# Converting weight pairs in one piece ahead of the sums, in the first block of a two-layer MLP, and a border cast behind two copies

## The chip, the cores and the metric

The kernel runs on one core of a Trainium2 chip. The metric is the device time of one execution in microseconds. The engines are named by what they do: TensorE (PE in the rows; PEld are its weight loads), VectorE (DVE), ScalarE (ACT), GpSimd (POOL) and SyncE (SP), which here only issues DMAs.

## What is computed

The input is a sequence of 2 x 3008 tokens with 256 features. A spectral layer (a real Fourier transform along the sequence, a complex 256 x 256 product, a soft threshold, the inverse transform) is followed by two MLP layers, each with 2048 hidden features:

```python
def _moe_ref(x, w_in, w_out):
    h = x @ w_in
    g = h * (1.0 / (1.0 + np.exp(-1.702 * h)))
    return (g @ w_out).astype(np.float32)

x = attn_out.reshape(B * S, D)          # 6016 x 256
x = _moe_ref(x=x, **moe_kwargs)
return _moe2_ref(x=x, **moe2_kwargs)    # the same with h * sigmoid(h)
```

The MLP weights arrive as 64-bit floating point numbers, seen as int64. The chip's engines do not compute in that type, so the kernel converts them with shifts and masks.

## The kernel before, in words

**Stages.** The forward transform, the middle product and the inverse transform come first; then the MLP. The conversion of the weights is spread over all of them. The tokens are cut into blocks of 1024 (the last has 896), and a block into two halves h of 512. `group(l, i, p)` does layer l, block i and a pair p of chunks of 128 hidden features, p = 0 to 7. Every fp32 operand of a product is split into a high part (rounded) and a remainder, and each product is three matmuls of 512 columns: high x high, high x remainder, remainder x high.

**A group.** The first layer's product of a pair is done with seven products in place of eight, by the Strassen-Winograd scheme: sums of input pieces (`xprep` 0 to 6) times sums of weight pieces (slots 0 to 6 of `w_in`). In the text they go by their piece of the input: X0 and Y1, then Z3 and X4, then X5 and Z6, then X2; X, Z, Y are three PSUM banks, of four. ScalarE copies a bank to SBUF (L791, L801, L803), VectorE adds another bank to that (L793, L809, L812), and the four results (y1 to y4) go through a gate: the activation (L775), a cast to the high part (L777), and `rest`, the remainder (L782), on VectorE for one of the four and on GpSimd for three. The second layer's products (L744, `out_next`) take these with a lag of four, that is a group later. Seven first-layer products and eight second-layer ones, of three matmuls each, make 45 matmuls a group. X5 and Z6 write banks that L801 and L803 must have read.

**Converting a pair of weights.** `cv_load` starts the DMA of a raw pair (L144, L145 or L148); there is one raw buffer. `cv_bits` begins with ScalarE (L157) and puts five steps of VectorE on the list `fill`, L162 to L166; L164 and L166 read the raw buffer, L166 last. `pump(k)` issues k of the steps, all without a number. `settle` adds the two parts (L219, on GpSimd). A kept pair of `w_in` is then placed in the next group by `place_in`: four sums on VectorE (L194 to L197, into the one buffer `tmp`), then two `put`s, each a cast on ScalarE and a remainder on GpSimd (both at L98 and L99): the pair itself (`cv_a`, 384 columns) and the sums (`tmp`, 512). A pair of `w_out` has one cast and one remainder (`place_out`). Pairs that cannot be kept yet are written to DRAM (`spilled`) and fetched again later (`cv_ld`).

**Which groups convert.** `WEIGHTS` lists the pairs with the mark `kept`; ten are converted before the MLP. In the first block of layer 1 (l = 0, i = 0) the groups p = 1 to 6 convert one pair each, all six kept: three of `w_in` and three of `w_out`. In blocks 1 to 4 the groups p = 1, 3, 5 and 6 convert one each (`kr`), sixteen in all, none kept. In the first block's groups p = 0 to 4 a spilled pair of `w_out` is placed too.

**What sets the order.** `hook(h)`, h = 1 to 6, is called at fixed points of a group and inserts what belongs there: at 1 the conversion's start (L157), at 2 and 3 placings of fetched weights, at 3 (or 1) the placing of converted ones, at 4 the rest of `fill` and the next raw load, at 5 a fetch, at 6 `settle`. From the group (0, 0, 1) on the order of the program is the order on every engine; group (0, 0, 0) and what lies beside it are ordered by a scheduler. Each engine, and each DMA queue, works in order. In group p = 0 of every block `xprep` 4, 6 and 5 (a cast on ScalarE, L692, and a remainder on VectorE, L695) are done in the group itself, at hooks 1, 2 and 3; the first four were done in the group before.

The lines at which the steps of the conversion are split up:

```python
        rest(nc.gpsimd, *gate(0, 0, y1))
        hook(2)
        pump(3)
```

Of the kernel before, what the change touches and what calls it, by code (L numbers as in the profile page):

```python
# [56 lines left out]
def spectral_mlp_kernel(ctx, tc, xin, m0, mfwd, minv, wc, bias, w_in1, w_out1, w_in2, w_out2, outT):  # L57
    nc = tc.nc
# [6 lines left out]
    def E(site, i=0):  # L65
        s = CFG.get(site, DEF[site])
        return {"V": nc.vector, "P": nc.gpsimd}[s[i % len(s)]]
# [135 lines left out]
    wib_p = []  # L203
# [12 lines left out]
    def settle():  # L216
        pump()
        for u, (a, c) in bits:
            E('cva', u[2]).tensor_add(a, a, c)  # L219
            if not u[3]:  # L220
                spilled[u[:3]] = d = dram_p.tile([P, 2 * CU], F32, name=f"w_{u[0]}{u[1]}_{u[2]}")
                nc.sync.dma_start(out=d, in_=a)
        fresh = [(u, a) for u, (a, _) in bits if u[3]]
        done, added[:] = added[:], fresh
        bits[:] = []
        return done

    def window(k, done, now=False):
        for u, a in done:
            if u[0] == "in":  # L230
                for part in place_in(u[1], u[2], a, E('pil', u[2]), sums_tmp):
                    if now:
                        for f in part:
                            f()
                    else:
                        fill.extend(part)
            else:
                place_out(u[1], u[2], a, E('pol', u[2]))
        for _ in range(min(k, len(loaded))):
            u, raw = loaded.pop(0)  # L240
            bits.append((u, cv_bits(raw)))
# [518 lines left out]
    def group(l, i, p, hook):  # L760
        t0, n = blocks[i]
        func = AF.Silu if l else AF.Gelu_apprx_sigmoid
        w = w_in[l, p]

        y = [[yt[:, mm, t0 + h * n : t0 + (h + 1) * n] for h in range(2)] for mm in range(2)]

        def prod(ps, s, k, first=True):

            xh, xl = xb[l, i, k]
            a, z = w[:, 0, s], w[:, 1, s]  # L770
            for m, (st, mv) in enumerate(((a, xh), (a, xl), (z, xh))):
                nc.tensor.matmul(ps, st, mv, start=first and m == 0, stop=m == 2, skip_group_check=True)  # L772

        def gate(row, h, g, src=None):
            nc.scalar.activation(g, g if src is None else src, func)  # L775
            gh = slot(1, F32R, "g")[:, :n]
            nc.scalar.copy(gh, g)  # L777
            return row, h, g, gh

        def rest(eng, row, h, g, gh):  # L780
            gl = slot(1, F32R, "g")[:, :n]
            eng.tensor_sub(gl, g, r32(gh))  # L782
            pend.append((l, i, p, row, h, gh, gl))

        (y1, y3), (y2, y4) = y
        begun = (l, i, p) != (0, 0, 0)
        X, Z, Y = (bank(0, "x")[:, :n] for _ in range(3))
        prod(X, 0, 0)  # L790
        nc.scalar.copy(y1, X)  # L791
        prod(Y, 1, 1)
        nc.vector.tensor_add(y1, y1, Y)  # L793
        hook(1)
        if begun:
            out_next()
        rest(nc.gpsimd, *gate(0, 0, y1))
        hook(2)
        pump(3)
        prod(Z, 3, 2)  # L800
        nc.scalar.copy(y2, Z)  # L801
        prod(X, 4, 3, False)
        nc.scalar.copy(y3, X)  # L803
        hook(3)
        if begun:
            out_next()
            out_next()
        prod(X, 5, 4, False)
        nc.vector.tensor_add(y2, y2, X)  # L809
        g22 = gate(1, 1, y2)  # L810
        prod(Z, 6, 6, False)
        nc.vector.tensor_add(y3, y3, Z)  # L812
        rest(nc.vector, *g22)
        g12 = gate(0, 1, y3)
        rest(nc.gpsimd, *g12)
        hook(4)
        if begun:
            out_next()
        hook(5)
        prod(X, 2, 5, False)  # L820
        rest(nc.gpsimd, *gate(1, 0, y4, X))
        hook(6)
# [25 lines left out]
    puts = []  # L848
# [12 lines left out]
    for at, (l, i, p) in enumerate(seq):  # L861
# [10 lines left out]
        def hook(h):  # L872
            if more:
                if h in (1, 2):
                    for x in ((0,), (1, 2))[h - 1]:
                        xprep(*nxt, x)
                if h == 3:
                    xprep(*nxt, 3, 1)
                if h == 4:
                    xprep(*nxt, 3, 2)  # L880
            if p == 0 and h < 4:
                xprep(l, i, {1: 4, 2: 6, 3: 5}[h])
            if h == 1 and p == NPR - 2 and (l, i) != (1, last):
                xsums(*nxt)
            if h == (3 if len(done) < 2 else 1):
                window(0, done, True)
                done[:] = []
            if h == 1:
                window(k, ())
            if h in (2, 3):  # L890
                moved(h)
            if h == 5:
                fetched[:] = fetch_for(at + 1)
            if h == 4:
                pump()
                cv_load(1 - len(loaded))
            if h == 6:
                done.extend(settle())
                done.extend(added)
                added[:] = []  # L900
# [159 lines left out]
```

## Time and profile before

| what | value |
|---|---|
| runs | 1248.66, 1251.43, 1253.36 us; median 1251.43 |
| the profiled execution | 1253.26 us, its span 1251.5 us |
| TensorE busy | 1187.8 us (95% of the span) |
| ScalarE, VectorE, GpSimd busy | 775.6, 698.2, 587.8 us |
| mean granted TensorE clock | 0.985 of full speed |

The span is the time from the first to the last instruction; the profiled execution's time is 1.8 us longer. Busy shares are means over stages with different limits: the transforms take some 220 us, the rest is the MLP. A busy TensorE is not TensorE at its peak, since matmuls overlap and their ends are modelled.

### The profile page before, as it was taken

How to read it: one execution, taken by the hardware profiler on the slowest of the kernel's cores; microseconds unless marked ns; L12 is line 12 of the kernel's file. 1: busy time of each engine (PE TensorE's matmuls, PEld its weight loads, DVE VectorE, ACT ScalarE, POOL GpSimd, SP SyncE). 2: the span in 40 equal slices, each digit the busy share in tenths (PEclk: the TensorE clock that was granted, in tenths of full speed). 3: DMA queues.
4: the chain of work that ended last, by engine and by line, in shares of the span. 5: the costliest groups of instructions: out<-in, count | busy, mean ns of one | idle time of the engine just before them, and what ended most of it. 6: DMA issues, size and time to landing. Idle time of an engine off the chain costs nothing.

```text
span 1251.5 us, 14934 instructions
## 1 busy us (share of the span) xinstructions
PE 1187.8 (95%) x5220; PEld 969.8 (77%) x5220; DVE 698.2 (56%) x1034; ACT 775.6 (62%) x1481; POOL 587.8 (47%) x465
## 2 busy tenths in 40 slices
PE   7879888777999999999999999999999999999998
PEld 4868678556787887887878987878888888888897
DVE  7899999866735646447446463352352442623522
ACT  3555433656766766767667777666675665765764
POOL 4585553555544444445455774433333333333342
PEclk9989989988999999999999999999999999999999
DMA  8452123011011001001011110000000000000000
GB/s 310 161 183 68 51 71 129 25 46 39 17 49 44 26 34 52 26 26 52 26 59 35 34 43 26 1 32 3 1 35 1 1 34 1 19 16 1 34 1 30
DMA packets 27277, 57.57 MB, mean 46 GB/s; under 512 B 2369, under 2 KB 11585, under 8 KB 25922
## 3 DMA queue, kind: packets, MB, share of 16 engines
q1 hardware_dynamic: 25154, 41.94, 10.2%
q0 software_dynamic: 2048, 14.68, 3.2%
q8 instruction: 41, 0.67, 0.2%
q14 instruction: 34, 0.28, 0.1%
HBM read 44.94 MB, written 11.67 MB: 45 GB/s over the span
## 4 chain that ended last, share of the span: by engine, by line
PE 71%; DVE 15%; ACT 6%; issue 3%; DMA 3%; POOL 1%; SPq 0%; DVEq 0%; ACTq 0%; POOLq 0%
PE o L744 37%; PE x L772 32%; ACT yt L775 1%; DVE f L533 1%; DVE fl L99 1%; PE psf L357 1%; DMA raw<-in_wi 1%; DMA raw<-in_wo 1%; DVE th L519 1%; ACT g L777 1%; DVE cv_c L166 1%; DVE cv_c L165 1%; DVE yt L664 1%; DVE g L782 1%; DVE cv_a L164 1%
## 5 line engine op out<-in xcount | busy, mean ns | idle before, releaser
L782 POOL TENSOR_TENSOR g<-yt,g 128x512 fp32r<-128x512 f32 (+1 forms) x288 | 384.5, 1347 | 538.6 <-DVE g L782 167.5
L744 PE MATMUL o<-g,wo 128*128 128x512 f32 (+1 forms) x2304 | 575.1, 392 | 1.0 <-POOL g L782 0.8
L772 PE MATMUL x<-x,wi 128*128 128x512 f32 (+1 forms) x2016 | 514.0, 394 | 26.5 <-ACT yt L803 22.1
L744 PEld LDWEIGHTS o<-g,wo 128*128 128x128 f32 x2304 | 434.0, 188 | 97.0 <-POOL g L782 1.2
L772 PEld LDWEIGHTS x<-x,wi 128*128 128x128 f32 x2016 | 378.0, 189 | 118.4 <-ACT yt L803 27.8
L775 ACT ACTIVATE yt<-yt 128x512 f32<-128x512 f32 (+1 forms) x288 | 178.9, 621 | 263.4 <-DVE yt L809 216.8
L777 ACT CAST g<-yt 128x512 fp32r<-128x512 f32 (+1 forms) x384 | 234.2, 612 | 11.8
L809 DVE TENSOR_TENSOR yt<-yt,x 128x512 f32<-128x512 f32 (+1 forms) x96 | 64.7, 674 | 264.1 <-PE x L772 264.1
L793 DVE TENSOR_TENSOR yt<-yt,x 128x512 f32<-128x512 f32 (+1 forms) x96 | 64.7, 674 | 143.2 <-ACT yt L791 142.2
L782 DVE TENSOR_TENSOR g<-yt,g 128x512 fp32r<-128x512 f32 (+1 forms) x96 | 68.8, 717 | 69.5 <-ACT g L777 68.5
L695 DVE TENSOR_TENSOR x<-yt,x 128x512 fp32r<-128x512 f32 (+1 forms) x48 | 53.5, 1114 | 24.2 <-ACT x L692 24.2
L812 DVE TENSOR_TENSOR yt<-yt,x 128x512 f32<-128x512 f32 (+1 forms) x96 | 64.8, 675 | 1.9 <-PE x L772 0.5
L775 ACT ACTIVATE yt<-x 128x512 f32<-128x512 f32 (+1 forms) x96 | 56.0, 584 | 3.7 <-PE x L772 3.7
L791 ACT COPY yt<-x 128x512 f32<-128x512 f32 (+1 forms) x96 | 54.8, 571 | 2.6 <-PE x L772 2.5
L803 ACT COPY yt<-x 128x512 f32<-128x512 f32 (+1 forms) x96 | 55.6, 579 | 0.6 <-PE x L772 0.6
L801 ACT COPY yt<-x 128x512 f32<-128x512 f32 (+1 forms) x96 | 54.7, 570 | 0.0
L219 POOL TENSOR_TENSOR cv_a<-cv_a,cv_c 128x512 f32<-128x512 f32 x32 | 47.0, 1469 | 15.9 <-DVE cv_c L166 12.4
L360 PE MATMUL psi<-m,fh 128*128 128x376 f32 (+3 forms) x208 | 49.8, 329 | 2.6 <-DVE sd L514 2.1
L157 ACT ACTIVATE cv_c<-raw 128x512 f32<-128x512 f32 x32 | 21.6, 674 | 43.8 <-DMA raw<-in_wo 23.7
L501 PE MATMUL psm<-wc_hi,xtl 128*128 128x512 f32 x96 | 38.6, 407 | 5.3 <-DVE xtl L99 5.3
L501 PE MATMUL psm<-wc_hi,xth 128*128 128x512 f32 x96 | 39.5, 412 | 3.7 <-ACT xth L98 3.7
L360 PE MATMUL psi<-m,fl 128*128 128x376 f32 (+3 forms) x104 | 34.8, 334 | 6.1 <-DVE fl L99 5.2
(108 smaller groups left out, 1065.7 us busy)
## 6 DMA issues: line engine op xcount, KB each, us to landing
raw<-in_wi SPq DMA_DIRECT2D x32, 256.0 KB, 3.1
raw<-in_wo SPq DMA_DIRECT2D x16, 512.0 KB, 3.6
raw<-in_x SPq DMA_DIRECT2D x12, 512.0 KB, 6.6
out_t<-yt SPq DMA_DIRECT2D x20, 256.0 KB, 2.0
m<-in_mf POOLq DMA_DIRECT2D x4, 1128.0 KB, 7.4
m<-in_mi POOLq DMA_DIRECT2D x4, 1128.0 KB, 7.6
w_out<-cv_a SPq DMA_DIRECT2D x13, 256.0 KB, 2.0
cv_ld<-w_out SPq DMA_DIRECT2D x13, 256.0 KB, 2.6
```

Source lines behind the costliest of these rows:

```text
L360: nc.tensor.matmul(ps, a, z, start=i == 0 and x == 0, stop=i == last and x == 2)
L501: nc.tensor.matmul(t, a, w, start=(n == 0), stop=(n == 11 and grp == 1))
L744: nc.tensor.matmul(acc[h, mm], st, mv, start=first and k == 0, stop=last and k == 2)
L772: nc.tensor.matmul(ps, st, mv, start=first and m == 0, stop=m == 2, skip_group_check=True)
L775: nc.scalar.activation(g, g if src is None else src, func)
L777: nc.scalar.copy(gh, g)
L782: eng.tensor_sub(gl, g, r32(gh))
L791: nc.scalar.copy(y1, X)
L793: nc.vector.tensor_add(y1, y1, Y)
L803: nc.scalar.copy(y3, X)
L809: nc.vector.tensor_add(y2, y2, X)
L812: nc.vector.tensor_add(y3, y3, Z)
```

## The change

It has four parts. In a group of the first block that converts a kept pair (`here`), two steps of `fill` are issued behind the first gate, the remainder of that gate goes to VectorE in place of GpSimd, and the three other steps follow at once; `pump()` without a number is also what groups of later blocks now do, which had three steps there and two at hook 4. `settle` does the sum L219 of kept pairs on VectorE, once the MLP has begun. `window`, when it places at once, does the four sums, then the put of `tmp`, then that of `cv_a`. And in p = 0 of each block `xprep` 6 moves from hook 2 to hook 3, ahead of `xprep` 5, which puts its cast behind the two copies of the banks.

```diff
--- before.py
+++ after.py
@@ -216,7 +216,7 @@
     def settle():
         pump()
         for u, (a, c) in bits:
-            E('cva', u[2]).tensor_add(a, a, c)
+            (nc.vector if wib_p and u[3] else E('cva', u[2])).tensor_add(a, a, c)
             if not u[3]:
                 spilled[u[:3]] = d = dram_p.tile([P, 2 * CU], F32, name=f"w_{u[0]}{u[1]}_{u[2]}")
                 nc.sync.dma_start(out=d, in_=a)
@@ -228,12 +228,12 @@
     def window(k, done, now=False):
         for u, a in done:
             if u[0] == "in":
-                for part in place_in(u[1], u[2], a, E('pil', u[2]), sums_tmp):
-                    if now:
-                        for f in part:
-                            f()
-                    else:
-                        fill.extend(part)
+                sums, puts = place_in(u[1], u[2], a, E('pil', u[2]), sums_tmp)
+                if now:
+                    for f in (*sums, *puts[::-1]):
+                        f()
+                else:
+                    fill.extend(sums + puts)
             else:
                 place_out(u[1], u[2], a, E('pol', u[2]))
         for _ in range(min(k, len(loaded))):
@@ -794,9 +794,14 @@
         hook(1)
         if begun:
             out_next()
-        rest(nc.gpsimd, *gate(0, 0, y1))
+
+        here = bool(bits) and bits[0][0][3]
+        g11 = gate(0, 0, y1)
+        if here:
+            pump(2)
+        rest(nc.vector if here else nc.gpsimd, *g11)
         hook(2)
-        pump(3)
+        pump()
         prod(Z, 3, 2)
         nc.scalar.copy(y2, Z)
         prod(X, 4, 3, False)
@@ -878,8 +883,9 @@
                     xprep(*nxt, 3, 1)
                 if h == 4:
                     xprep(*nxt, 3, 2)
-            if p == 0 and h < 4:
-                xprep(l, i, {1: 4, 2: 6, 3: 5}[h])
+            if p == 0:
+                for x in {1: (4,), 3: (6, 5)}.get(h, ()):
+                    xprep(l, i, x)
             if h == 1 and p == NPR - 2 and (l, i) != (1, last):
                 xsums(*nxt)
             if h == (3 if len(done) < 2 else 1):
```

Lines behind L794 move by five: L801, L803, L809 and L812 of the kernel before are L806, L808, L814 and L817 now. The texts below use the numbers of before.

VectorE, first block, from the start of a pair's conversion in p = 3 (raw_2514 is the pair; cv_a, cv_c and tmp are its parts, g a gate, x the banks). Before:

```order
L162 TENSOR_SCALAR cv_c<-cv_c 128x512
L163 TENSOR_SCALAR cv_c<-cv_c 128x512
L164 SCALAR_TENSOR_TENSOR cv_a<-raw_2514,cv_c 128x512
L194 TENSOR_TENSOR tmp<-cv_a 128x128
L195 TENSOR_TENSOR tmp<-cv_a 128x128
L196 TENSOR_TENSOR tmp<-tmp,cv_a 128x128
L197 TENSOR_TENSOR tmp<-cv_a,tmp 128x128
L809 TENSOR_TENSOR yt<-yt,x 128x512
L812 TENSOR_TENSOR yt<-yt,x 128x512
L782 TENSOR_TENSOR g<-yt,g 128x512
L165 TENSOR_SCALAR cv_c<-cv_a 128x512
L166 SCALAR_TENSOR_TENSOR cv_c<-raw_2514,cv_c 128x512
```

Now:

```order
L162 TENSOR_SCALAR cv_c<-cv_c 128x512
L163 TENSOR_SCALAR cv_c<-cv_c 128x512
L782 TENSOR_TENSOR g<-yt,g 128x512
L164 SCALAR_TENSOR_TENSOR cv_a<-raw_2514,cv_c 128x512
L165 TENSOR_SCALAR cv_c<-cv_a 128x512
L166 SCALAR_TENSOR_TENSOR cv_c<-raw_2514,cv_c 128x512
L194 TENSOR_TENSOR tmp<-cv_a 128x128
L195 TENSOR_TENSOR tmp<-cv_a 128x128
L196 TENSOR_TENSOR tmp<-tmp,cv_a 128x128
L197 TENSOR_TENSOR tmp<-cv_a,tmp 128x128
L814 TENSOR_TENSOR yt<-yt,x 128x512
L817 TENSOR_TENSOR yt<-yt,x 128x512
```

L165 and L166 stand ahead of the sums and of both additions, and the first gate's L782 stands among the steps.

ScalarE, first block, from p = 1 into p = 2 (raw_2410 is the pair that p = 2 converts; wi and wo are placings, L775 and L777 gates). Before:

```order
L98 CAST wi_2364<-tmp 128x512
L98 CAST wo<-cv_ld 128x512
L791 COPY yt<-x 128x512
L775 ACTIVATE yt<-yt 128x512
L777 CAST g<-yt 128x512
L775 ACTIVATE yt<-yt 128x512
L777 CAST g<-yt 128x512
L775 ACTIVATE yt<-x 128x512
L777 CAST g<-yt 128x512
L157 ACTIVATE cv_c<-raw_2410 128x512
```

Now:

```order
L791 COPY yt<-x 128x512
L98 CAST wi_2366<-tmp 128x512
L98 CAST wi_2366<-cv_a 128x384
L98 CAST wo<-cv_ld 128x512
L775 ACTIVATE yt<-yt 128x512
L157 ACTIVATE cv_c<-raw_2410 128x512
L775 ACTIVATE yt<-yt 128x512
L777 CAST g<-yt 128x512
```

Here L157 stands ahead of all but one of the gate instructions of p = 1, which it followed before, and L791 of p = 2 ahead of the casts. From p = 3 on L157 keeps its place on ScalarE, and only the casts of tmp and cv_a change places.

GpSimd, first block, from the two last gates of p = 2 to the placings of p = 3. Before:

```order
L782 TENSOR_TENSOR g<-yt,g 128x512 x2
L219 TENSOR_TENSOR cv_a<-cv_a,cv_c 128x512
L782 TENSOR_TENSOR g<-yt,g 128x512
L99 TENSOR_TENSOR wi_2570<-cv_a,wi_2570 128x384
L99 TENSOR_TENSOR wi_2570<-tmp,wi_2570 128x512
```

Now:

```order
L782 TENSOR_TENSOR g<-yt,g 128x512 x2
L99 TENSOR_TENSOR wi_2572<-tmp,wi_2572 128x512
L99 TENSOR_TENSOR wi_2572<-cv_a,wi_2572 128x384
L99 TENSOR_TENSOR wo<-cv_ld,wo 128x512
L782 TENSOR_TENSOR g<-yt,g 128x512 x2
```

GpSimd has nothing between the last gates of one group and the placing of the next.

## Rows read from the trace of the kernel before

**Rows 1.** The page, part 4: the chain that ended last, by engine.

```profile
PE 71%; DVE 15%; ACT 6%; issue 3%; DMA 3%; POOL 1%; SPq 0%; DVEq 0%; ACTq 0%; POOLq 0%
```

**Rows 2.** Waits of TensorE, 240 to 330 us, then 330 to 700: total, times, longest.

```profile
PE x L772 <- ACT yt L803: 16.5, 4, 5.1
...
PE x L772 <- ACT yt L803: 3.7, 4, 2.0
```

**Rows 3.** Stretches: length, busy time (instructions) of PE, PEld, DVE, ACT, POOL, clock, DMA.

```profile
268.91:284.81 15.90, 11.35 (x45) 8.13 (x46) 10.68 (x14) 8.23 (x16) 9.25 (x8) 0.99 0.17 50
...
300.69:312.84 12.15, 12.15 (x45) 9.69 (x46) 7.97 (x11) 7.92 (x14) 8.06 (x7) 0.86 0.13 44
312.84:323.34 10.50, 10.50 (x46) 8.45 (x45) 7.99 (x10) 7.79 (x14) 6.77 (x5) 1.00 0.17 52
```

**Rows 4.** Timeline of TensorE: start, length, work, in brackets the wait before it.

```profile
253.16 2.93 PE L772 MATMUL x<-x,wi 128*128 128x512 f32 x6 [5.10 <-ACT yt L803]
...
300.69 2.19 PE L772 MATMUL x<-x,wi 128*128 128x512 f32 x6 [3.70 <-ACT yt L803]
...
312.84 1.56 PE L772 MATMUL x<-x,wi 128*128 128x512 f32 x6
...
484.04 1.67 PE L772 MATMUL x<-x,wi 128*128 128x512 f32 x6 [1.98 <-ACT yt L803]
...
752.97 1.67 PE L772 MATMUL x<-x,wi 128*128 128x512 f32 x6 [1.44 <-ACT yt L803]
```

**Rows 5.** The chain of waits in order of time, 240 to 320 us.

```profile
260.77 1.68 DVE cv_c L166
262.93 3.04 DMA raw<-in_wi
266.06 0.67 ACT cv_c L157
267.73 0.69 DVE cv_a L164
268.42 1.29 DVE tmp L194
...
275.09 1.45 DVE cv_c L165
```

**Rows 6.** Timeline of ScalarE.

```profile
250.31 0.66 ACT L157 ACTIVATE cv_c<-raw 128x512 f32<-128x512 f32 x1 [6.53 <-DMA raw<-in_wi]
...
271.30 0.62 ACT L98 CAST wi<-tmp 128x512 fp32r<-128x512 f32 x1 [2.03 <-DVE tmp L197]
...
272.34 0.63 ACT L775 ACTIVATE yt<-yt 128x512 f32<-128x512 f32 x1
...
275.86 0.58 ACT L791 COPY yt<-x 128x512 f32<-128x512 f32 x1
...
751.34 0.61 ACT L692 CAST x<-yt 128x512 fp32r<-128x512 f32 x1
```

**Rows 7.** Timeline of VectorE.

```profile
234.25 0.28 DVE L194 TENSOR_TENSOR tmp<-cv_a 128x128 f32<-128x128 f32 x1
...
278.15 0.68 DVE L793 TENSOR_TENSOR yt<-yt,x 128x512 f32<-128x512 f32 x1
...
303.81 0.69 DVE L782 TENSOR_TENSOR g<-yt,g 128x512 fp32r<-128x512 f32 x1
304.42 0.42 DVE L165 TENSOR_SCALAR cv_c<-cv_a 128x512 uint32<-128x512 uint32 x1
304.87 0.69 DVE L166 SCALAR_TENSOR_TENSOR cv_c<-raw,cv_c 128x512 f32<-128x512 uint32 x1
...
472.37 0.69 DVE L809 TENSOR_TENSOR yt<-yt,x 128x512 f32<-128x512 f32 x1 [3.15 <-PE x L772]
```

**Rows 8.** Timeline of GpSimd.

```profile
274.89 2.79 POOL L782 TENSOR_TENSOR g<-yt,g 128x512 fp32r<-128x512 f32 x2 [0.35 <-ACT g L777]
```

## The prediction

> **What bounds the kernel now.** I read the chain of waits first. TensorE carries 71% of the chain that ends last [rows 1]: most of the span is matmuls back to back, which this change does not touch. What it can touch has to be found by place. TensorE's waits between 240 and 330 us [rows 2] put 16.5 us on one pair: a first-layer product (L772) that waits for ScalarE's copy of its bank (L803), four times, all in the first block; four more between 330 and 700 us make 3.7. The table by stretches [rows 3] cuts from one such product to the next, from group p=3 to 4, 5 to 6 and 6 to 7: 15.90, 12.15 and 10.50 us for the same 45 or so matmuls. So 10.5 us is TensorE's own pace, and a group of 15.9 loses 5.4. The timeline of TensorE [rows 4] shows the first of these waits (5.10 us, p=2).
>
> Why the copy is late is in the chain [rows 5]: L166 ends the use of the raw pair (there is one raw buffer), the next load starts and takes 3.04 us, L157 reads it, VectorE does L164 and the sums, and only a gate later L165 and L166, which closes the ring. From the end of L166 (262.45) to L157 (266.06) are 3.6 us. ScalarE works in order, so its first gate and the copies L801 and L803 stand behind L157. The reader is to see that the load is not slow: it is asked for late, because L165 and L166 stand behind the second half of the group.
>
> **The change part by part.**
> *All five steps ahead of the sums.* In the groups that convert a kept pair (p=1 to 6 of the first block) L162 to L166 now follow the first gate, and the load can start there. The load's new ring: L157 0.67 [rows 5], a gate with its cast 1.17 (three fill 272.34 to 275.86 [rows 6]), L782 0.69, L164 0.69, L165 0.42, L166 0.69 [rows 5, 7], load 3.6: 7.9 us. That is below 10.5, so the wait for the load goes. SP's queue keeps its order; the fetch that stands ahead of a load waits for GpSimd's placing in the group before, which is earlier.
>
> *What is late next.* With the load gone a second ring decides, in which ScalarE and VectorE hand work to each other: the cast of tmp waits for the four sums, these for L166, that for L782, and that for the gate. One round: the cast of cv_a 0.5 (an estimate, from the cast of tmp, 0.62 for 512 columns, to its 384); the casts of tmp and wo and three gates, 271.30 to 275.86, 4.56; the copy L791 0.58 [rows 6]; the addition L793 0.68 [rows 7]; one gate 1.17; L782 0.69, L164 0.69, L165 0.42, L166 0.69; four sums of 0.28 [rows 7], 1.12. Together 11.1 us, just above TensorE's 10.5. I take it for the three steps from p=2 to p=5; p=5 and 6 place an output pair, without sums and with one cast, and fall back to 10.5.
>
> *GpSimd left idle.* L782 of the first gate and the sum L219 move from GpSimd to VectorE: 0.69 there for L782 (in the ring above), and I take the same for L219, a two-input instruction of the same shape. GpSimd took 2.79 for two L782 [rows 8]. L219 stands in VectorE's slack behind the second gate. Beside GpSimd VectorE is slow: L165 took 1.45 where alone it took 0.42, L166 1.68 for 0.69, L194 1.29 for 0.28 [rows 5, 7]; a collision costs about 1.0 us. In the new order GpSimd ends the former group's two L782 soon after L791 and gets nothing until the cast of tmp, so L782 to the sums run alone. GpSimd has five instructions a group; between none and five collisions a round the ring lies from 11.1 to 16.1 us. I take none, since the rows without collision are those with GpSimd idle, as it is here.
> The Trainium skill, page "SBUF — State Buffer", section "Who interferes with whom", says that VectorE and GpSimd share a pair of ports which is locked for a whole instruction, and that the second to come is blocked. The rows agree: a step beside a GpSimd instruction of 1.4 us takes 1.0 us more. By that rule alone all five could hold the ring up; this is a rival below.
>
> *The sum for the first block.* From p=2 to p=6 the products stand at 253.16 [rows 4] and 312.84 [rows 3]: 59.7 us. After: 3 x 11.1 + 10.5 = 43.8. Saved 15.9. Bounds: 10.5 four times (17.7 saved), and two collisions, a ring of 13 us (10.2 saved).
> The way into p=2: ScalarE waited there until 250.31 for its pair [rows 6]. On VectorE the pair before gets its L166 earlier, past four sums (1.1) and two additions (1.4), and without the collisions of L165 and L166 (2.0): the load lands 4.5 us or more earlier. But in ScalarE's new order this L157 stands ahead of the three gates of p=1 (3.5 us), which the old wait had behind it. At least 1.0 is left, at most the whole wait of 5.1; I take 2.0, near the lower end, where the rows lead. Bounds 0 and 5.1.
>
> *Later blocks.* In blocks 1 to 4 a pair follows a pair in neighbouring groups once each (p=5, then 6), and there the same wait stands, the longest 1.98 us [rows 4], 3.7 for the four [rows 2]. GpSimd keeps its L782 there, but L165 and L166 move ahead of the addition for which VectorE idles (3.15 us before it [rows 7]), so the load starts some 4 us earlier. The four waits go, and about 0.1 each for the restart: 4.1. Bounds 2.1 and 4.1. In the sixteen groups of these blocks that convert, the two steps cost 1.1 alone and 3.1 with collisions: that idle time covers either, and I charge nothing. Without that cover it would be up to 3.1 us of VectorE a group, still with the next product's start in between.
>
> *The border cast* (of b22, in p=0 of every block) goes behind the two copies. It can free only a copy that TensorE waits for: one clear case, 1.44 us at 752.97 [rows 4], with that 0.61 us cast just ahead of the copies [rows 6]. The product X5 gets its bank some 0.5 earlier, but Z6 then waits for the remainder of the moved cast, which comes as much later. I take 0; bounds 0.5 saved, 1 lost. The exchanged order of the two placements (tmp first) is in the ring already.
>
> **Sum.** 15.9 + 2.0 + 4.1 = 22.0. Against the profiled execution's 1253.26 that is 1231.3. The median of the runs shown, 1251.43, lies 1.8 lower, which would make 1229.4; I forecast 1230, between the two.
>
> **The rivals.**
> *A longer ring (1239).* Two collisions a round, 13 us, and nothing gained on the way into p=2: 10.2 + 4.1 saved. For it: GpSimd's two L782 reach into the time of L162, and L219 now meets them. Against: L162 and L163 have about half a microsecond of slack to the gate.
> *The port eats it (1248).* Five collisions a round: 3 x 16.1 + 10.5 = 58.8, 0.9 saved, and 4.1 in the later blocks. For it: today several steps of a round do collide [rows 5]. Against: those lie where GpSimd works, and the new places are others.
> *The load does not start earlier (1253).* Then the change does not do what it says, because something ahead of the load in SP's queue holds it. Against: the chain goes from L166 straight into the load [rows 5].
> *TensorE's clock (1268, slower).* Granted clocks were 0.99, 0.86 and 1.00 of 2.4 GHz [rows 3]. The stretch of 12.15 us begins right after a wait of 3.70 [rows 4] and ran in part at the lower level, 1.2 GHz. If short waits in each round kept TensorE there, six matmuls would take 2.93 us, as at 253.16, instead of 1.56 [rows 4], a group 10.5 x 2.93 / 1.56 = 19.7, and four of them 78.9 instead of 59.7: 19.2 lost, less the 4.1. It decides from about 16 us a group on. Against: a stretch that loses 5.4 us to waiting was still granted 0.99 [rows 3], and the new ring leaves only 0.6 us a group.
>
> **How the numbers follow.** Forecast 0.78, longer ring 0.12, port 0.05, load not earlier 0.02, clock 0.03. The first two lie below 1245.2, that is faster by over 0.5% (6.3 us, about what a measurement of this kernel can tell from no change): 0.90. Port and load are within 0.5%: 0.07. Slower: 0.03. For the range the best ends, 17.7 + 5.1 + 4.1 + 0.5 = 27.4, and the median's 1.8 give 1224; the longer ring with half the later blocks' gain, 12.3 saved, gives 1241. I say 1223 to 1241, which leaves out about the last three rivals.
>
> **What would show it.** Right: in the first block L157 no longer waits for a load; the products X5 of p=2 to 5 stand some 11 us apart; L164 to L197 take their short times; ScalarE's waits there are for tmp (L197); and the waits at p=6 of blocks 1 to 4 are gone. Wrong: L157 still behind a load, VectorE's steps at 1.4 us and more, a group over 13 us, a product Z6 that waits at p=0, or a lower granted clock between 250 and 300 us than now.

## The result and the profile after

| | before | changed |
|---|---|---|
| median of the runs made together, us | 1251.93 (4 runs, 1248.66 to 1253.36) | 1234.16 (4 runs, 1233.39 to 1236.81) |
| profiled execution, its span, us | 1253.26, 1251.5 | 1233.84, 1232.1 |
| granted clock of TensorE, 252 to 296 us | 0.90 | 1.00 |

The changed kernel is faster: ratio 0.9865, 95% interval 0.9841 to 0.989. The forecast was 1230.0 us, range 1223 to 1241.

Where the 19.4 us between the two spans come from, read at the products X5 as in the prediction:

| stretch | before, us | changed, us | saved | forecast |
|---|---|---|---|---|
| ahead of the first change (the same work) | | | 2.1 | not forecast |
| way into p=2 | to 253.16 | to 250.27 | 0.8 | 2.0 |
| X5 of p=2 to X5 of p=6, first block | 59.68 | 44.18 | 15.5 | 15.9 |
| X5 of p=6 to the end of the span | 938.66 | 937.65 | 1.0 | 4.1 |

The first row is a difference between two executions of the same instructions (ScalarE's third copy stands at 225.90 before and at 223.82 after in the first group), and no gain of the change: in the kernels of the experiments the same copy stands anywhere from 223.47 to 226.02. Without that row the change gave 17.3 us between these two executions, and 17.8 by the medians, where the forecast's sum had 22.0. The forecast missed by 4 us on the two rows where it took waits away outside the ring.

Waits of TensorE in the changed kernel (total, times, longest), 222 to 335 us, then 335 to 1240:

```profile
PE o L744 <- POOL wo L99: 3.3, 3, 1.9
PE x L772 <- ACT yt L791: 1.6, 1, 1.6
PE x L772 <- DVE yt L793: 1.5, 1, 1.5
...
PE x L772 <- ACT yt L808: 2.0, 5, 0.9
PE x L772 <- DVE x L695: 1.3, 3, 0.6
```

The 16.5 us behind the copy L803 [rows 2] are gone from the first block (L808 is the same copy in the changed kernel); what is left there are 7.8 us of other waits. In the later blocks the waits are shorter, but new ones have come.

The stretches from product to product, p=3 to 4, 4 to 5 and 5 to 6 (columns as in [rows 3]):

```profile
261.04:272.50 11.46, 10.77 (x46) 8.37 (x45) 9.33 (x16) 8.28 (x15) 7.12 (x5) 1.00 0.28 70
272.50:283.95 11.45, 10.77 (x46) 8.37 (x45) 9.35 (x15) 8.79 (x16) 7.90 (x6) 1.00 0.15 47
283.95:294.45 10.50, 10.50 (x46) 8.45 (x45) 8.12 (x13) 7.33 (x13) 3.70 (x4) 1.00 0.19 51
```

A group that took 15.90 takes 11.46, at a clock of 1.00, and the last one runs at TensorE's own 10.50, where the forecast had 11.1 and 10.5. That last gain is one of the clock: TensorE was busy all through this group before too, but at 0.86, and needed 12.15 [rows 3]. The round from p=2 to p=3 is 10.77 at X5, because X5 of p=2 itself comes late (below); between ScalarE's third copies it is 11.63 (247.43 to 259.06), about as long as the others.

One round on VectorE (timeline; what answers to [rows 5, 7]):

```profile
268.13 0.69 DVE L793 TENSOR_TENSOR yt<-yt,x 128x512 f32<-128x512 f32 x1 [0.38 <-ACT yt L791]
268.74 0.46 DVE L162 TENSOR_SCALAR cv_c<-cv_c 128x512 f32<-128x512 f32 x1
269.23 1.41 DVE L163 TENSOR_SCALAR cv_c<-cv_c 128x512 uint32<-128x512 uint32 x1
270.56 0.68 DVE L782 TENSOR_TENSOR g<-yt,g 128x512 fp32r<-128x512 f32 x1
271.16 0.68 DVE L164 SCALAR_TENSOR_TENSOR cv_a<-raw,cv_c 128x512 uint32<-128x512 uint32 x1
271.88 0.43 DVE L165 TENSOR_SCALAR cv_c<-cv_a 128x512 uint32<-128x512 uint32 x1
272.34 0.69 DVE L166 SCALAR_TENSOR_TENSOR cv_c<-raw,cv_c 128x512 f32<-128x512 uint32 x1
272.95 0.28 DVE L194 TENSOR_TENSOR tmp<-cv_a 128x128 f32<-128x128 f32 x1
```

and on ScalarE and GpSimd, apart, the rows that tell who waits:

```profile
242.11 0.67 ACT L157 ACTIVATE cv_c<-raw 128x512 f32<-128x512 f32 x1 [0.80 <-DMA raw<-in_wi]
...
262.54 0.62 ACT L98 CAST wi<-tmp 128x512 fp32r<-128x512 f32 x1 [2.89 <-DVE tmp L197]
...
268.00 0.68 ACT L157 ACTIVATE cv_c<-raw 128x512 f32<-128x512 f32 x1
...
279.45 0.68 ACT L157 ACTIVATE cv_c<-raw 128x512 f32<-128x512 f32 x1
```

```profile
242.17 1.28 POOL L99 TENSOR_TENSOR wo<-cv_ld,wo 128x512 fp32r<-128x512 f32 x1
...
267.17 3.18 POOL L782 TENSOR_TENSOR g<-yt,g 128x512 fp32r<-128x512 f32 x2
```

L157 no longer waits for a load, but for 0.80 us once; it waited 6.53 [rows 6]. ScalarE now waits for tmp, as foreseen. L782 to the sums run at their short times. One collision is left on the ring: L163 takes 1.41 beside the two L782 of GpSimd, where alone it takes 0.43.

The Trainium skill, page "SBUF — State Buffer", section "Who interferes with whom", says that a VectorE instruction of the tensor_scalar kind can enter a two-port mode and then contends with GpSimd for the shared ports, and that whichever issues first holds them for its whole instruction. The rows agree: L163 has one input tile and lost 1.0 us, and GpSimd's pair of L782 took 3.18 here and 2.62 in the kernel of the first experiment below.

### The profile page after: what moved, and what is told of

It reads as the page before. It is cut to its first block, busy times and chain, and to the rows that moved or that the text cites. A ratio compares the mean times of both kernels' runs of the same rounds, so it can differ in the third digit from the quotient of the medians.

```text
span 1232.1 us, 14937 instructions
## 1 busy us (share of the span) xinstructions
PE 1185.0 (96%) x5220; PEld 967.0 (78%) x5220; DVE 696.9 (57%) x1046; ACT 775.9 (63%) x1481; POOL 564.4 (46%) x453
## 3 DMA queue, kind: packets, MB, share of 16 engines
q1 hardware_dynamic: 25154, 41.94, 10.5%
HBM read 44.94 MB, written 11.67 MB: 46 GB/s over the span
## 4 chain that ended last, share of the span: by engine, by line
PE 66%; DVE 17%; ACT 8%; issue 5%; DMA 2%; POOL 1%; SPq 0%; DVEq 0%; ACTq 0%; POOLq 0%
PE o L744 35%; PE x L772 31%; ACT yt L775 3%; ACT g L777 2%; DVE fl L99 1%; DVE f L533 1%; DVE cv_a L164 1%; DVE th L519 1%; DVE yt L664 1%; DMA raw<-in_x 1%; DVE xl L320 1%; DVE cv_c L162 1%; DVE yt L793 1%; DVE cv_c L165 1%; DVE cv_c L163 1%
## 5 line engine op out<-in xcount | busy, mean ns | idle before, releaser
L782 POOL TENSOR_TENSOR g<-yt,g 128x512 fp32r<-128x512 f32 (+1 forms) x282 | 367.9, 1318 | 531.5 <-DVE g L782 278.2
L775 ACT ACTIVATE yt<-yt 128x512 f32<-128x512 f32 (+1 forms) x288 | 179.1, 622 | 279.1 <-DVE yt L814 231.5
L777 ACT CAST g<-yt 128x512 fp32r<-128x512 f32 (+1 forms) x384 | 234.2, 612 | 11.7
L814 DVE TENSOR_TENSOR yt<-yt,x 128x512 f32<-128x512 f32 (+1 forms) x96 | 64.6, 673 | 229.4 <-PE x L772 229.2
L793 DVE TENSOR_TENSOR yt<-yt,x 128x512 f32<-128x512 f32 (+1 forms) x96 | 64.8, 675 | 162.7 <-ACT yt L791 154.7
L782 DVE TENSOR_TENSOR g<-yt,g 128x512 fp32r<-128x512 f32 (+1 forms) x102 | 70.9, 695 | 75.0 <-ACT g L777 75.0
L695 DVE TENSOR_TENSOR x<-yt,x 128x512 fp32r<-128x512 f32 (+1 forms) x48 | 47.0, 979 | 35.6 <-ACT x L692 35.6
L817 DVE TENSOR_TENSOR yt<-yt,x 128x512 f32<-128x512 f32 (+1 forms) x96 | 64.7, 674 | 0.8
L775 ACT ACTIVATE yt<-x 128x512 f32<-128x512 f32 (+1 forms) x96 | 56.2, 586 | 2.2 <-PE x L772 2.2
L808 ACT COPY yt<-x 128x512 f32<-128x512 f32 (+1 forms) x96 | 55.7, 580 | 0.9 <-PE x L772 0.9
L791 ACT COPY yt<-x 128x512 f32<-128x512 f32 (+1 forms) x96 | 54.9, 572 | 2.1 <-PE x L772 2.1
L806 ACT COPY yt<-x 128x512 f32<-128x512 f32 (+1 forms) x96 | 54.9, 572 | 0.0
L219 POOL TENSOR_TENSOR cv_a<-cv_a,cv_c 128x512 f32<-128x512 f32 x26 | 38.5, 1479 | 13.4 <-DVE cv_c L166 9.9
L360 PEld LDWEIGHTS psi<-m,fh 128*128 128x128 f32 x208 | 38.1, 201 | 2.8 <-DVE sd L514 2.5
```

What stands on the lines that cost most here:

```text
L360: nc.tensor.matmul(ps, a, z, start=i == 0 and x == 0, stop=i == last and x == 2)
```

## The experiments

Each experiment starts from the kernel before or from the changed one, as its text says. Lines are those of the experiment's own kernel, a few off where lines were added. A "step" is the distance from one first-block L157 to the next, p=4 to p=5 unless the text says otherwise; it is 15.90 before (266.06 to 281.96) and 11.45 changed (268.00 to 279.45).

### What carries the first block: order, GpSimd or copies

**Steps ahead alone.**

```diff
-        rest(nc.gpsimd, *gate(0, 0, y1))
+        here = bool(bits) and bits[0][0][3]
+        g11 = gate(0, 0, y1)
+        if here:
+            pump(2)
+        rest(nc.gpsimd, *g11)
         hook(2)
-        pump(3)
+        pump(None if here else 3)
```

> The kernel before with one part of the change: in first-block groups that convert a kept pair, two steps behind the first gate and all the rest behind the second hook; the remainder of g11 and the addition of a and c stay on GpSimd, the later blocks keep three steps, the copies their order. Theory (the one raw buffer is asked for late, and GpSimd's company costs 1.0 us a step): the order alone brings most, but two or three steps of a ring still run beside GpSimd, at +1.0 us each, so the four steps from p=2 to p=6 come to 13 us rather than 15.9 (before) or 11.5 (changed): about 1240 us. Rival A (only the company of GpSimd costs): the steps stay near 15.9, 1250 us. Rival B (only the order counts): steps of 11.5, 1234 to 1236 us.

Measured: 1242.49 us, ratio 0.9929 (0.9914 to 0.9944); a step of 12.50. ScalarE, VectorE, then GpSimd, in that kernel:

```profile
269.69 0.68 ACT L157 ACTIVATE cv_c<-raw 128x512 f32<-128x512 f32 x1
282.19 0.68 ACT L157 ACTIVATE cv_c<-raw 128x512 f32<-128x512 f32 x1
```

```profile
271.17 1.41 DVE L163 TENSOR_SCALAR cv_c<-cv_c 128x512 uint32<-128x512 uint32 x1
272.67 1.61 DVE L164 SCALAR_TENSOR_TENSOR cv_a<-raw,cv_c 128x512 uint32<-128x512 uint32 x1
```

```profile
270.81 1.48 POOL L219 TENSOR_TENSOR cv_a<-cv_a,cv_c 128x512 f32<-128x512 f32 x1
272.25 1.49 POOL L782 TENSOR_TENSOR g<-yt,g 128x512 fp32r<-128x512 f32 x1
```

The order alone gives 3.4 of the 4.45 us a step, and L157 waits for no load any more. GpSimd's instructions follow one another beside L163 and L164 (and L165, 1.13 in the round before), so 1.0 us a step is left. Both rivals fall. The time is 2.5 us above the 1240 that I expected, though the step is shorter: from the third copy of p=6 to the end this profile has 944.20 us, where the kernel before has 940.07. No run was made on that.

**GpSimd idle alone.**

```diff
-        rest(nc.gpsimd, *gate(0, 0, y1))
+        here = bool(bits) and bits[0][0][3]
+        rest(nc.vector if here else nc.gpsimd, *gate(0, 0, y1))
...
-            E('cva', u[2]).tensor_add(a, a, c)
+            (nc.vector if wib_p and u[3] else E('cva', u[2])).tensor_add(a, a, c)
```

> The kernel before with the other part: the remainder of g11 in converting groups of the first block and the addition of a and c for kept pairs on VectorE, nothing else moved; three steps behind the second hook as before. Theory: the three steps of the ring that ran 1.0 us longer beside GpSimd (L166, L165, L194 of the rows) run at their own length, and 0.7 us comes on VectorE: steps of 15.9 - 3.0 + 0.7 = 13.6 us, 1242 us. Rival A (only GpSimd's company costs): steps of 11.5 to 12, 1234 to 1237 us. Rival B (only the order counts): steps of 15.9 or more, 1250 to 1254 us.

Measured: 1255.27 us, ratio 1.003 (1.0018 to 1.0041); a step of 16.35. My number missed; rival B, that only the order counts, was the nearest. VectorE in that kernel:

```profile
271.71 1.34 DVE L164 SCALAR_TENSOR_TENSOR cv_a<-raw,cv_c 128x512 uint32<-128x512 uint32 x1
...
277.73 1.52 DVE L165 TENSOR_SCALAR cv_c<-cv_a 128x512 uint32<-128x512 uint32 x1
279.28 1.67 DVE L166 SCALAR_TENSOR_TENSOR cv_c<-raw,cv_c 128x512 f32<-128x512 uint32 x1
```

L165 and L166 still meet GpSimd's remainders of the other gates, which were not moved; only the sums run clear. In exchange L782, which waits for a gate behind L157, now stands on VectorE ahead of L162, and L164 meets the remainder of cv_a. An instruction taken off GpSimd is no gain by itself: this part is a loss of 3.6 us alone, and 0.8 us a step are gained by it behind the new order (the run after the next).

**Copies and border cast alone** (the sums' pieces are put first, the cast of piece 6 goes behind hook 3):

```diff
-                for part in place_in(u[1], u[2], a, E('pil', u[2]), sums_tmp):
...
+                sums, puts = place_in(u[1], u[2], a, E('pil', u[2]), sums_tmp)
+                if now:
+                    for f in (*sums, *puts[::-1]):
+                        f()
...
-                xprep(l, i, {1: 4, 2: 6, 3: 5}[h])
+                for x in {1: (4,), 3: (6, 5)}.get(h, ()):
+                    xprep(l, i, x)
```

> The kernel before with only the two small parts: the copies of the sums' pieces ahead of the other three, and the border cast of piece 6 behind hook 3. Theory: neither lies on the ring before the change (ScalarE waits there for the load): 1251 us, within 1 us. Rival: the order of the copies shortens the ring by 0.5 us a step, 1249 us; or the border cast is late for its product and costs 0.4 to 0.6 us at a border, 1252 us and a new wait of TensorE on VectorE's remainder at p=0.

Measured: 1250.66 us over ten runs, ratio 0.9994 (0.9981 to 1.0007): no difference that the times can tell. The profiled execution does have a shorter step, 14.60 (L157 at 263.50 and 278.10): with cv_a's remainder later on GpSimd, L195 takes 0.28 where it took 1.10 in the kernel before, and the second gate's L782 0.74 where it took 1.43. So neither my sentence that the copies lie off the ring nor the rival's 0.5 us fits that trace. How much of it is in every execution stays open.

**The changed kernel with the copies back.**

```diff
-                    for f in (*sums, *puts[::-1]):
+                    for f in (*sums, *puts):
```

> The changed kernel with the copy of the other three pieces (cv_a) ahead of that of the sums' pieces, as before. Theory (company of GpSimd costs more than the cast): the cast of 0.52 us fits in ScalarE's wait of 2.9 us for the sums, but its remainder on GpSimd (1.0 us or more) then runs beside L164 to L194 on VectorE and lengthens one or two of them by 0.65 to 1.0 us each, on the ring: steps of 11.6 to 12.9 in place of 11.46, 1235 to 1240 us. Rival (the cast is all that counts): steps of 10.9 to 11.0, 1232 us.

Measured: 1235.28 us (1234.64 to 1235.53), ratio 0.9875 (0.9861 to 0.989); a step of 11.67, at the lower end of what was expected. VectorE and GpSimd in that kernel:

```profile
262.12 1.39 DVE L166 SCALAR_TENSOR_TENSOR cv_c<-raw,cv_c 128x512 f32<-128x512 uint32 x1
```

```profile
261.69 1.27 POOL L99 TENSOR_TENSOR wi<-cv_a,wi 128x384 fp32r<-128x384 f32 x1 [2.22 <-DVE cv_a L164]
```

The cast does fit into ScalarE's wait, but its remainder meets L166. The copies' order is worth 0.2 us a step here; the first round gains more (12.42 between the third copies, 11.63 in the changed kernel), which makes 1.2 us for the three. The two ranges of times do overlap. The chain of the three parts is then, per step: 15.90 before, 12.50 with the order, 11.67 with GpSimd idle too, 11.45 with the copies turned round.

### Is the load in the ring

**The loads left out, in the kernel before and in the changed one.**

```diff
+            if wib_p and kept and held:
+                loaded.append(((kind, l, p, kept), held[0]))
+                continue
             raw = cv_p.tile([P, 2 * CU], mybir.dt.int64, tag="raw", name="raw64", bufs=1)
+            held[:] = [raw]
```

> The kernel before, leaving out the loads of kept pairs for groups p=2 to p=6 of the first block (the steps work on the values that the raw buffer already holds; all else is as before). Theory (a step before is the load's ring: L166, load, L157, L162 to L164, sums, casts, gates, L165, L166): ScalarE's wait of 5 us before L157 goes, the next bound is ScalarE and VectorE in turn, with the collisions that stay: steps of 12.0 to 13.0, 1236 to 1241 us. Rival A (the company of GpSimd is the bound, and the load hides behind it): steps of 15 or more, 1248 us or more. Rival B (a whole gain without any reordering): 11.5, 1234 us.

> The changed kernel, leaving out the same loads. Theory (no step from p=3 on runs through the load any more; only the first L157 waits 0.8 us for it): steps of 11.4 to 11.5 as with the loads, 0 to 1 us less in all, 1233 to 1234 us. Rival (the load is still in the ring, or its traffic slows the steps): 1225 to 1230 us.

Measured: 1236.16 us without the loads in the kernel before, ratio 0.9886 (0.9869 to 0.9902); 1234.93 us in the changed one, 0.9872 (0.9858 to 0.9887), against 1234.16 with its loads. L157 (it is L162 in both) in the first, then in the second:

```profile
267.32 0.68 ACT L162 ACTIVATE cv_c<-raw 128x512 f32<-128x512 f32 x1
279.87 0.67 ACT L162 ACTIVATE cv_c<-raw 128x512 f32<-128x512 f32 x1
```

```profile
269.55 0.68 ACT L162 ACTIVATE cv_c<-raw 128x512 f32<-128x512 f32 x1
281.02 0.68 ACT L162 ACTIVATE cv_c<-raw 128x512 f32<-128x512 f32 x1
```

Without loads the old order makes a step of 12.55, the same as the new order with loads and with GpSimd at work (12.50), whose L157 waits for none. So the order's gain in a step is the load's wait; that the two kernels also lose the same amount to collisions is not shown. In the changed kernel a step is 11.47 without the loads and 11.45 with them, and the times show no gain either: the load is out of the ring.

The second of these also speaks on the way into p=2. TensorE waits there with no load at all:

```profile
245.12 2.08 PE L749 MATMUL o<-g,wo 128*128 128x512 f32 x4 [2.39 <-POOL wo L99]
```

In the changed kernel the same wait is 1.94 us:

```profile
243.50 1.27 PE L744 MATMUL o<-g,wo 128*128 128x512 f32 x4 [1.94 <-POOL wo L99]
244.57 2.76 PE L772 MATMUL x<-x,wi 128*128 128x512 f32 x6
```

```profile
244.57:250.27 5.70, 5.70 (x19) 4.51 (x18) 4.26 (x8) 3.13 (x6) 2.64 (x2) 0.71 0.17 45
```

The output pair's remainder is third on GpSimd, behind those of tmp and cv_a, which wait for the sums of p=1. It was third before too, with a wait of 0.17; but in the new order these sums stand behind all five steps of their own pair. The last of them ends at 239.19 and before at 237.95, which is 3.3 us later once the 2.1 us of the table's first row are taken off. The wait has a second price: behind it TensorE was granted 0.71, and six matmuls took 2.76 where the same six took 1.56 before (243.69), at a clock of 1.00. No kernel was run that moves only this.

### Where the later blocks' gain went

The distance from ScalarE's third copy in p=2 of a block to that in the next block's p=2 (L803 before, L808 in the others), us; eight groups at TensorE's pace are 84.0 (the last column ends two smaller groups of block 5 further on and is shorter by that):

| kernel | block 1 | block 2 | block 3 | block 4 |
|---|---|---|---|---|
| before | 84.87 | 86.24 | 84.90 | 83.48 |
| changed | 84.85 | 84.84 | 84.87 | 83.41 |
| three steps in all later groups | 84.89 | 85.13 | 84.83 | 83.70 |
| three steps at p=6 alone | 83.99 | 84.00 | 84.00 | 82.82 |

The waits at p=6 are gone, and yet blocks 1, 3 and 4 are as long as before. Changed kernel, block 1, TensorE at p=7, then VectorE at p=6, then ScalarE at p=7:

```profile
390.26 1.67 PE L772 MATMUL x<-x,wi 128*128 128x512 f32 x6 [0.20 <-ACT yt L808]
```

```profile
380.27 0.43 DVE L165 TENSOR_SCALAR cv_c<-cv_a 128x512 uint32<-128x512 uint32 x1
380.73 0.69 DVE L166 SCALAR_TENSOR_TENSOR cv_c<-raw,cv_c 128x512 f32<-128x512 uint32 x1
381.34 0.68 DVE L814 TENSOR_TENSOR yt<-yt,x 128x512 f32<-128x512 f32 x1
```

```profile
388.10 0.62 ACT L692 CAST x<-yt 128x512 fp32r<-128x512 f32 x1
388.62 0.62 ACT L692 CAST x<-tmp 128x512 fp32r<-128x512 f32 x1
...
389.62 0.59 ACT L808 COPY yt<-x 128x512 f32<-128x512 f32 x1
```

L165 and L166 stand in front of the addition L814, and L814 starts 2.32 us after its product X5 (379.02). In the kernel before the same addition (L809 there) started 1.08 us after X5:

```profile
397.79 1.67 PE L772 MATMUL x<-x,wi 128*128 128x512 f32 x6 [0.60 <-ACT yt L803]
398.87 0.69 DVE L809 TENSOR_TENSOR yt<-yt,x 128x512 f32<-128x512 f32 x1 [1.32 <-PE x L772]
```

ScalarE's gates follow L814, so ScalarE comes to p=7 that much later, and there the casts for the next block stand ahead of the copy L808. Two kernels test this.

**Three steps again in all groups of the later blocks.**

```diff
-        pump()
+        pump(None if here else 3)
```

> The changed kernel with three steps behind the second hook again in all groups that convert no kept pair (the later blocks), the first block as changed. Theory from the two profiles (from p=2 of one block to p=2 of the next the changed kernel is 1.40 us shorter in block 2 and 0.0 to 0.1 in blocks 1, 3 and 4): the waits at p=6 return (0.6, 2.0, 0.6, 0.5 us), those at p=7 go, and the time is 1.4 to 1.6 us longer than the changed kernel's. Rival, as forecast (the waits at p=6 are the whole of it): 3.5 to 4 us longer.

Measured: 1235.40 us (1235.03 to 1235.44), ratio 0.9873 (0.9856 to 0.9889), 1.2 us more than the changed kernel, which lies inside that kernel's range; TensorE waits 2.6 us in four places for L808 between 335 and 700 us. The four blocks of the table are 0.6 us longer than in the changed kernel. The waits at p=6 return as the theory said, the forecast's 3.5 to 4 us do not, and my 1.4 to 1.6 was too much as well. In block 2 ScalarE waits 2.85 us for the load at p=6, where it waited 3.99 in the profile of before: part of the 1.98 us [rows 4] was a load that landed late in that execution.

**Three steps at p=6 of blocks 1 to 4 alone.**

```diff
-        pump()
+        pump(3 if i and p == 6 else None)
```

> The changed kernel, with three steps behind the second hook in group p=6 of blocks 1 to 4 alone; p=5 of those blocks keeps all of them. Theory (why the later blocks gave so little: with all steps ahead at p=6, L165 and L166 push the addition L814 back by 1.2 us, the ScalarE chain of the group runs late by that, and at p=7, where the casts for the next block come in, TensorE waits instead): the load of p=6 is still asked for early at p=5, L814 of p=6 comes without delay, and both waits are gone. 0.6 to 0.8 us less in each of four blocks, 2.4 to 3.2 us less than the changed kernel: 1231 to 1232 us; no TensorE wait over 0.1 us at p=6 or p=7 of blocks 1 to 3. Rival A (the casts at the border are late by themselves): as the changed kernel, 1234 us, waits at p=7 unchanged. Rival B (the next load matters): p=6 waits return, 1235.5 us.

Measured: 1230.49 us (1230.27 to 1231.18), ratio 0.9839 (0.9824 to 0.9853). VectorE, then TensorE, in that kernel:

```profile
380.64 0.68 DVE L814 TENSOR_TENSOR yt<-yt,x 128x512 f32<-128x512 f32 x1
...
383.35 0.42 DVE L165 TENSOR_SCALAR cv_c<-cv_a 128x512 uint32<-128x512 uint32 x1
383.81 0.69 DVE L166 SCALAR_TENSOR_TENSOR cv_c<-raw,cv_c 128x512 f32<-128x512 uint32 x1
```

```profile
379.49 1.56 PE L772 MATMUL x<-x,wi 128*128 128x512 f32 x6
...
389.99 1.56 PE L772 MATMUL x<-x,wi 128*128 128x512 f32 x6
```

From X5 of p=6 to X5 of p=7 it is 10.50, TensorE's pace, and there is no wait at either. The four blocks are 3.2 us shorter than in the changed kernel (table). At p=5 the two steps belong ahead, since the next group converts and needs the raw buffer; at p=6 the next pair is wanted only in p=1 of the next block, and there they only cost.

**The border cast back** (the changed kernel with piece 6 behind hook 2):

```diff
-                for x in {1: (4,), 3: (6, 5)}.get(h, ()):
-                    xprep(l, i, x)
+                xprep(l, i, {1: 4, 2: 6, 3: 5}[h])
```

> The changed kernel with the cast of piece 6 behind hook 2 again, as before. Theory from the profiles so far (the kernels with the cast behind hook 3 show TensorE waits of 0.3 to 0.6 us on VectorE's remainder at three borders, and 0.5 us less at the border of block 5 to 6): 0.1 to 0.4 us less than the changed kernel, nothing that the times can tell, and no wait of TensorE on the remainder of a piece (VectorE, x) from 335 us on. Rival, as forecast (the cast moved costs or gives nothing): equal within 0.1 us in the trace from block to block.

Measured: 1234.58 us (1233.73 to 1235.89), ratio 0.9864 (0.9844 to 0.9883): the times tell nothing. The three waits for the remainder (1.3 us, listed above) are gone, and at one border the wait behind L808 is 1.44 in place of 0.93. From p=2 of block 1 to the last group it is 0.55 us shorter in the profile: the moved cast costs a little.

### Trying to shorten the ring that is left

**The second remainder on VectorE, then that with the border cast back, then that with the casts ahead.** All three have three steps at p=6.

```diff
-        rest(nc.gpsimd, *g12)
+        rest(nc.vector if here else nc.gpsimd, *g12)
```

> The kernel of the run with three steps at p=6, and in the converting groups of the first block the remainder of g12 on VectorE too. Theory (the one collision left on the ring is L163 beside GpSimd's two remainders in a row, 1.41 in place of 0.43 us; with one remainder there, GpSimd is done before L163 starts; VectorE pays 0.7 us in front of L793, of which 0.4 us is its wait there): steps 0.3 to 0.7 us shorter, 10.8 to 11.2 us, 1 to 3 us less than that kernel, 1228 to 1230 us. Rival (VectorE's time is the ring): steps 0.3 us longer, 1232 us.

> The same with the cast of piece 6 behind hook 2 as before: 0.1 to 0.4 us less than the run with the second remainder, whatever that gives.

Measured: 1230.91 us (1230.55 to 1231.60), ratio 0.9834 (0.9816 to 0.9852), and 1230.51 us (1230.15 to 1231.47), 0.9833 (0.9811 to 0.9854). In the first, VectorE:

```profile
278.36 1.25 DVE L782 TENSOR_TENSOR g<-yt,g 128x512 fp32r<-128x512 f32 x1 [0.45 <-ACT g L777]
...
280.73 0.93 DVE L162 TENSOR_SCALAR cv_c<-cv_c 128x512 f32<-128x512 f32 x1
281.69 0.43 DVE L163 TENSOR_SCALAR cv_c<-cv_c 128x512 uint32<-128x512 uint32 x1
```

L163 is clear, as meant, but the moved remainder meets GpSimd itself and L162 takes 0.93. A step is 11.28, only 0.2 less, and the step before it, p=3 to p=4, is 12.39, where the kernel with three steps at p=6 has 11.42: over the three rounds nothing is gained, and the times show nothing. With the border cast back the profile is 0.5 us shorter from p=2 of block 1 on, as in the run above; the times show nothing of that either.

The last one puts the casts of cv_a and of the fetched pair ahead of the sums, with their remainders where they were:

```diff
-                    for f in (*sums, *puts[::-1]):
+                    for f in (puts[0], *early, *sums, *puts[1:], *late):
                         f()
```

> The kernel of the run with second remainder and border cast, and in the first block's groups the casts of cv_a and of the fetched output pair ahead of ScalarE's wait for the sums, their remainders on GpSimd left where they were (behind that of tmp). Theory (the ring is ScalarE and VectorE in turn, and the two casts of 0.51 and 0.62 us fill a wait of 2.9 us that is there anyway, without bringing GpSimd's remainders forward): steps of 11.3 - 1.1 = 10.2, held at TensorE's own 10.5, or up to 11.0 with one collision more at L162 to L164, since VectorE comes back earlier while GpSimd does not: 0.9 to 2.4 us less, 1228 to 1229.6 us. Rival (GpSimd's chain of three remainders and a gate's is now the bound, or collisions take it all back): steps of 11.3 or more, 1230.5 us.

Measured: 1230.85 us (1230.74 to 1233.85), ratio 0.9833 (0.9813 to 0.9854). ScalarE's wait for the sums is 1.58 in place of 2.89, but VectorE pays:

```profile
267.31 3.11 DVE L794 TENSOR_TENSOR g<-yt,g 128x512 fp32r<-128x512 f32 x2 [0.66 <-ACT g L789]
270.35 1.78 DVE L230 TENSOR_TENSOR cv_a<-cv_a,cv_c 128x512 f32<-128x512 f32 x1
```

The two remainders and the addition (L794 and L230 there) meet GpSimd's chain of remainders. Between ScalarE's third copies this round takes 12.40 us and the next one 11.12; the rival had it. (This profile is of the longest of its five executions, 1233.85 us.) Moving an instruction within this ring moves the collision with it.

The kernel with three steps at p=6 alone is therefore the best found with one line of change: 1230.49 us, below both kernels.

## Why the prediction held, and where it did not

**The load is asked for late: right.** The forecast took the load out of the ring by the order of L165 and L166. Leaving the loads out gives the same step as that order does, 12.55 and 12.50, and in the changed kernel leaving them out makes it no faster.

**What is late next: right, and 0.35 us too short.** The forecast's round was 11.1; it is 11.45. The casts and gates up to L791 take 4.98 (262.54 to 267.52; forecast 5.06). The step that failed is "L162 and L163 have about half a microsecond of slack to the gate": with L163 at 1.41 the two take 1.82 us from 268.74 to 270.56, in place of the gate's 1.17 that the sum had there. The slack was there (the gate ends at 270.14), but it is half as long as a collision of 1.0. The premise behind "I take none", that GpSimd ends its two L782 "soon after L791", did not hold: they end at 270.35, 2.8 us after L791 starts. The other terms came out a little shorter, since an instruction's row overlaps the next by up to 0.1 us. L782 to the sums did run alone. The sum for the first block, 15.9, came out at 15.5, and that is nearer than its rounds were: read at ScalarE's third copies the three rounds take 34.55 in place of 33.3, and the late X5 of p=2, which is charged to the way into p=2, hides 0.9 of this.

**The way into p=2: 0.8 in place of 2.0.** The sum treated ScalarE's wait for its pair as the whole wait. The load did come earlier (L157 at 242.11, waiting 0.80), and the wait of 5.10 is gone. But TensorE then waited 0.58 for L814 and 1.94 for the output pair's remainder, whose placing the new order makes later, and ran at 0.71 behind these waits, some 1.5 us longer for the same matmuls. It waits there even without loads. The step named only the load and not what is late next behind it. That the sums behind five steps are the cause is read from the traces and was not tried.

**Later blocks: 1.0 in place of 4.1.** The waits went, as forecast. The failed step is "that idle time covers either, and I charge nothing". The row quoted there is of p=5, where VectorE is idle until its product comes; at p=6 the steps began late, behind the next block's sums and L162 at 1.51 us, and L165 and L166 ran past that product. What they cost appeared a group later, at p=7. Blocks 1 to 4 gave 1.5 us in the table, 1.4 of it in block 2. With three steps at p=6 the blocks give 3.2 us more, 4.2 in all: the size of the term was there, and the changed kernel takes three quarters of it back. Part of it, the longest wait, came with a load that landed late, which three of the six profiles of kernels with the old steps show.

**The border cast: 0 was near.** It costs about 0.55 us in the trace, inside the bounds; the wait at Z6 that the prediction named is there at three borders, 0.59 at the longest.

**The rivals.** The longer ring had 13 us; the order alone made 12.5, and it is the idle GpSimd and the turned copies that keep the changed kernel at 11.45. The port, the late load and the clock are excluded by the rows above: one collision a round on the ring, no L157 behind a load after p=2, and a granted clock of 1.00 from 252 to 296 us. There the clock went the other way: the longer waits of the kernel before went with 0.90 in that stretch. Only ahead of it, from 244.57 to 250.27, was the clock lower than before, which is part of the row above.

## What to carry to other kernels

When one buffer is refilled in a loop, look at which instruction frees it and how much unrelated work stands in front of that instruction; with the reordering alone a round here was as short as with no load at all. Put such steps ahead only in the groups whose successor needs the buffer: elsewhere they delay what follows on the same engine, and the bill comes a group later, where some other burst of work has used up the slack. When a wait is removed, read the distance between fixed points on both sides of it and not the list of waits: in three of four blocks here the wait went and the distance stayed.

## What the runs showed of the hardware beyond expectation

- Many instructions of VectorE and GpSimd get longer when they run together, both of them. L219 on VectorE took 0.68 alone (e.g. 244.71 in the changed kernel) and 1.76 to 1.78 beside GpSimd; L163 0.43 and 1.41; two L782 in a row on GpSimd 2.62 in the kernel with the steps ahead alone, and 3.18 beside L219 and L163 in the changed one. Not all do: the addition L793, which takes one of its inputs from a PSUM bank, took 0.69 in the middle of that same pair (268.13), and from 222 us on none of the additions L793, L809 and L812 of the kernel before, which all read a bank, took more than 0.69.
- Among those that do, the cost of a collision hardly depends on the kind of the VectorE instruction: +1.0 for one input tile (L163, L165), +1.0 for two (L166), +1.1 for the addition L219; partial overlaps cost 0.25 to 0.9 (L162 0.70 in the kernel with the steps ahead alone, L782 1.55 at 246.76 in the changed one).
- In the kernels that keep three steps, ScalarE's wait for the load at p=6 of block 2 was 3.99, 4.17 and 3.90 us in three profiles and 2.85, 2.85 and 3.02 in three others. What delays the load was not tried.
